# Opening of a fused attention and MLP kernel: replicating four scale vectors on TensorE instead of by DMA, adding beta by extra matmul rows, and loading q by head groups

## The chip, the cores and the metric

The kernel runs on one core of a Trainium2 chip. The metric is the device time of one execution in microseconds. "Span" is the length of the profiled execution, some 1.8 us less than the time of the same run (828.8 and 830.6 for the kernel before). Executions of one kernel on one chip differ by 0.3 to 0.5%. So stages are compared by their times inside the traces, and whole kernels by repeated runs beside the kernel before on the same chip.

## The reference

Eight batches, 16 query heads, 4 key heads, 384 positions, head size 64, model width 1024, hidden width 4096.

```python
scores = scale * np.matmul(q, k.transpose(0, 1, 3, 2))      # k, v repeated over the heads of a group
attn = softmax(scores)
x = np.matmul(attn, v)                                       # -> [8, 384, 1024]
a1 = alpha1 * x + beta1
tok = np.einsum('ts,bsd->btd', w_tok, a1)                    # "token mix"
u = x + lam * tok
a2 = alpha2 * u + beta2
ch = np.maximum(a2 @ w_ch1, 0.0) @ w_ch2                     # h, then ch
return u + lam * ch
```

## The kernel before

The kernel works batch by batch. `main(b)` is the two big products of batch b; `side(b+1)`, the attention and token mix of the next batch, is cut into units that are slipped between the matmuls of `main(b)`. The first batch has nothing to hide behind: `side(0)` runs alone. I call that stretch, up to the first `h` matmul, the **opening**, and `main(0)` with `side(1)` in it the **first big stage**.

The parts that the change touches, with cuts marked:

```python
def bcast(eng, t, ap, lo, hi):                 # one vector to all 128 partitions, by DMA
    src = bass.AP(tensor=ap.tensor, offset=ap.offset + lo, ap=[[0, P], [1, hi - lo]])
    eng.dma_start(out=t[:, lo:hi], in_=src)
# ... in av_piece(p, hh) of the first batch: lam is folded into alpha1 and beta1
nc.vector.tensor_tensor(out=g1[:, r], in0=g1[:, r], in1=lam_t[:, r], op=MUL)
nc.vector.tensor_tensor(out=h1[:, r], in0=h1[:, r], in1=lam_t[:, r], op=MUL)
# ... x = av / sum, then
nc.vector.tensor_tensor(out=t, in0=x[:, :, cols(p)], in1=bc(g1, p), op=MUL)          # L232
eng = nc.gpsimd if first and p < NP - 2 else nc.vector
eng.tensor_tensor(out=a1s[p], in0=t, in1=bc(h1, p), op=ADD)                          # L235
# ... tok(p)
for tt in range(NST):
    for st in range(NST):
        nc.tensor.matmul(out=ps[:, tt, :], lhsT=wtokT[:, st, tt * P:(tt + 1) * P],   # L242
                         rhs=a1s[p][:, st, :], start=(st == 0), stop=(st == NST - 1))
u = x[:, :, cols(p)]
nc.vector.tensor_tensor(out=u, in0=ps, in1=u, op=ADD)                                # L245
nc.vector.tensor_tensor(out=a2s[p], in0=u, in1=bc(al2, p), op=MUL)                   # L247
# ... head of the program
load_k(0)
nc.scalar.dma_start(out=qst, in_=...)          # q, first head group
load_q(0, [0], G)                              # q, the other groups, in pieces of 64 elements
load_q(0, [1, 2], G)
for t, ap in ((g1, moe_alpha1), (lam_t, moe_lam), (h1, moe_beta1)):
    bcast(nc.scalar, t, ap, 0, 256)
    bcast(nc.sync, t, ap, 256, DM)
bcast(nc.sync, al2, moe_alpha2, 0, DM)
for c in range(RING):
    load_w1(c)
```

The softmax here doesn't subtract the row's maximum and nothing guards it: scores larger than these inputs give would overflow.

Of the kernel before, what the change touches and what calls it, by code (L numbers as in the profile page):

```python
# [12 lines left out]
def kernel(  # L13
# [21 lines left out]
    nc = tc.nc  # L35
# [34 lines left out]
    g1, h1, lam_t, al2 = (const.tile([P, DM], f32, tag=n, name=n) for n in ("g1", "h1", "lam", "al2"))  # L70
# [12 lines left out]
    def load_k(b):  # L83
        ks[b] = []
        for h in range(0, Hkv, 2):
            t = sb.tile([P, 2, NST, D], f32, tag="kst", name="kst", bufs=2)
            nc.sync.dma_start(out=t, in_=k[b, h:h + 2].rearrange("h (p st) d -> p h st d", st=NST))
            ks[b].append(t)

    def place_k(b, i):  # L90
        if i == 0:
            k2s[b] = sb.tile([P, NST, Hkv, 2, D], bf, tag="k2", name="k2", bufs=1)
        copies = (nc.vector.tensor_copy, nc.vector.tensor_copy if i else nc.scalar.copy) if b < 2 else [nc.gpsimd.tensor_copy] * 2
        for a in range(2):
            copies[a](out=k2s[b][:, :, 2 * i:2 * i + 2, a, :], in_=ks[b][i].rearrange("p h st d -> p st h d"))
# [5 lines left out]
    def load_q(b, sts=range(NST), i=0):  # L101
        if b not in qrs:
            qrs[b] = sb.tile([P, NST, Hq, D], bf, tag="q_raw", name="q_raw", bufs=1)
        for st in sts:
            nc.gpsimd.dma_start(out=qrs[b][:, st, i:], in_=by_st(q[b])[:, st, i:])
# [8 lines left out]

    def bcast(eng, t, ap, lo, hi):
        src = bass.AP(tensor=ap.tensor, offset=ap.offset + lo, ap=[[0, P], [1, hi - lo]])
        eng.dma_start(out=t[:, lo:hi], in_=src)
# [16 lines left out]
    def tp_ps(shape):  # L134
        return psum.tile(shape, bf, tag="tp", name="tp", bufs=1)
# [6 lines left out]
    def side(b):  # L142
        vb = vt[b % 2]
        x = sb.tile([P, NST, DM], f32, tag="x", name="x", bufs=2)
        xs[b] = x
# [11 lines left out]
        def k_transpose(h0):  # L157
            k2 = k2s[b]
            ps = tp_ps([P, 2 * NST, P])
            for i in range(2 * NST):  # L160
                src = k2[:, i % NST, h0 + i // NST].rearrange("p a d -> p (a d)")
                nc.tensor.matmul(out=ps[:, i, :], lhsT=src, rhs=ident, is_transpose=True,
                                 start=(i == 0), stop=(i == 2 * NST - 1), skip_group_check=True)
            nc.vector.tensor_copy(out=kT[:, :, h0:h0 + 2, :].rearrange("p st h s -> p h st s"),
                                  in_=ps.rearrange("p (h st) s -> p h st s", h=2))

        def q_transpose(g):
            ps = tp_ps([P, 2 * NST, P])
            for i in range(2 * NST):
                h = g * G + 2 * (i // NST)  # L170
                nc.tensor.matmul(out=ps[:, i, :],  # L171
                                 lhsT=qrs[b][:, i % NST, h:h + 2, :].rearrange("p h d -> p (h d)"),
                                 rhs=ident, is_transpose=True, start=(i == 0),
                                 stop=(i == 2 * NST - 1), skip_group_check=True)
            nc.vector.tensor_copy(out=qT[:, :, 2 * g:2 * g + 2, :].rearrange("p st a s -> p a st s"),  # L175
                                  in_=ps.rearrange("p (a st) s -> p a st s", a=2))
# [3 lines left out]
        def scores(i, later=False):  # L180
# [11 lines left out]
            def exp():  # L192
                e = sb.tile([P, 2, 4, P], bf, tag="es", name="es", bufs=EB)
                nc.scalar.activation(out=e, in_=sc, func=EXP, scale=scale_qk)  # L194
                ess[i] = e
# [10 lines left out]
        def av_piece(p, hh):  # L206
# [12 lines left out]
            if hh == 0:  # L219
                if first and p in (0, 2):  # L220
                    r = slice(0, 256) if p == 0 else slice(256, DM)
                    nc.vector.tensor_tensor(out=g1[:, r], in0=g1[:, r], in1=lam_t[:, r], op=MUL)
                    nc.vector.tensor_tensor(out=h1[:, r], in0=h1[:, r], in1=lam_t[:, r], op=MUL)
                return
            rinv = sb.tile([P, 2, NST, 1], f32, tag="rinv", name="rinv", bufs=1)
            nc.vector.reciprocal(out=rinv, in_=av[:, :, :, D:])  # L226
            for hh in range(2):
                c0 = (2 * p + hh) * D
                nc.vector.tensor_tensor(out=x[:, :, c0:c0 + D], in0=av[:, hh, :, :D],  # L229
                                        in1=rinv[:, hh].to_broadcast([P, NST, D]), op=MUL)  # L230
            t = sb.tile([P, NST, P], f32, tag="tmp", name="a1f", bufs=4)
            nc.vector.tensor_tensor(out=t, in0=x[:, :, cols(p)], in1=bc(g1, p), op=MUL)  # L232
            a1s[p] = sb.tile([P, NST, P], bf, tag="a1", name="a1", bufs=2)
            eng = nc.gpsimd if first and p < NP - 2 else nc.vector
            eng.tensor_tensor(out=a1s[p], in0=t, in1=bc(h1, p), op=ADD)  # L235

        def tok(p):
            ps = psum.tile([P, NST, P], f32, tag="av" if first else "sc", name="tok",
                           bufs=1 if first else 2)
            for tt in range(NST):  # L240
                for st in range(NST):
                    nc.tensor.matmul(out=ps[:, tt, :], lhsT=wtokT[:, st, tt * P:(tt + 1) * P],  # L242
                                     rhs=a1s[p][:, st, :], start=(st == 0), stop=(st == NST - 1))
            u = x[:, :, cols(p)]
            nc.vector.tensor_tensor(out=u, in0=ps, in1=u, op=ADD)  # L245
            a2s[p] = sb.tile([P, NST, P], bf, tag="a2", name="a2", bufs=3)
# [15 lines left out]
        def wtok_transpose():  # L262
            wv = wtok_in.rearrange("p tt (s st) -> p tt st s", st=NST)
            for st in range(NST):
                ps = tp_ps([P, NST, P])
                for tt in range(NST):
                    nc.tensor.matmul(out=ps[:, tt, :], lhsT=wv[:, tt, st, :], rhs=ident,
                                     is_transpose=True, start=(tt == 0),
                                     stop=(tt == NST - 1), skip_group_check=True)
                nc.vector.tensor_copy(out=wtokT[:, st, :], in_=ps.rearrange("p a b -> p (a b)"))  # L270
# [10 lines left out]
        if not first:  # L281
            if pe_flip:
# [3 lines left out]
                add(q_transpose, 1)  # L286
            for j in range(NP + 4):
# [3 lines left out]
                if j <= NP:  # L291
                    add(scores2, j)
                    if pe_flip and j in (1, 3):
                        add(q_transpose, 2 + j // 2)
# [8 lines left out]
        add(q_transpose, 0)  # L303
        for i in range(18):
            add(scores, i)
            if i == 1:
                add(q_transpose, 1)
            if i in (5, 9):
                add(q_transpose, i // 4 + 1)
            if i == 4:  # L310
                add(k_transpose, 2)
            if i == 6:
                add(wtok_transpose)
            for p in range(NP):
# [4 lines left out]
                if i == last + 2 and p > 1:  # L319
                    add(tok_flip, p - 2)  # L320
        add(tok, NP - 3)
        add(av_piece, NP - 1, 0)
        add(av_piece, NP - 1, 1)
        add(tok, NP - 2)
        add(a2_transpose, NP - 3)
        add(tok, NP - 1)
        add(a2_transpose, NP - 2)
# [53 lines left out]
    with tc.manual_schedule(engines=order):  # L381

        nc.vector.memset(wtokT, 0.0)
        warm = psum.tile([P, 512], f32, tag="mm", name="warm", bufs=2)
        for _ in range(9):
            nc.tensor.matmul(out=warm[:, :S], lhsT=wtokT[:, 0, :P], rhs=wtokT[:, 1, :],
                             start=True, stop=True)
        load_k(0)
        stage = sb.tile([P, NST, DM], f32, tag="x", name="stage", bufs=2)
        qst = stage[:, 0, :G * NST * D].rearrange("p (h st d) -> p h st d", h=G, st=NST)  # L390
        nc.scalar.dma_start(out=qst, in_=q[0, :G].rearrange("h (p st) d -> p h st d", st=NST))
        load_q(0, [0], G)
        make_identity(nc, ident)
        for t in vt:
            nc.vector.memset(t[:, :, :, D:], 1.0)
        load_q(0, [1, 2], G)
        vst = stage[:, 2, :Hkv * NST * D].rearrange("p (h st d) -> p h st d", h=Hkv, st=NST)
        nc.sync.dma_start(out=vst, in_=v[0].rearrange("h (p st) d -> p h st d", st=NST))
        nc.gpsimd.tensor_copy(out=vt[0][:, :, :, :D], in_=vst.rearrange("p h st d -> p st h d"))
# [3 lines left out]
        load_k(1)  # L403
        for t, ap in ((g1, moe_alpha1), (lam_t, moe_lam), (h1, moe_beta1)):
            bcast(nc.scalar, t, ap, 0, 256)
            bcast(nc.sync, t, ap, 256, DM)
        bcast(nc.sync, al2, moe_alpha2, 0, DM)
        wtok_in = stage[:, 1, :NST * S // 2].bitcast(bf).rearrange("p (tt s) -> p tt s", tt=NST)
        nc.gpsimd.dma_start(out=wtok_in, in_=moe_w_tok.rearrange("(p tt) s -> p tt s", tt=NST))
        be2 = stage[:, 0, DM - NDT:]  # L410
        with nc.allow_non_contiguous_dma(reason="one small vector, once"):
            nc.sync.dma_start(out=be2, in_=moe_beta2.rearrange("(dt di) -> di dt", di=P))
        for c in range(RING):
            load_w1(c)
        loads = {7: [(load_w2, 0, 0, 2)], 25: [(load_q, 1, [0]), (load_q, 1, [1])],
                 31: [(load_q, 1, [2]), (load_v, 1, [0])], 37: [(load_v, 1, [1])], 43: [(load_v, 1, [2])]}
        for i, f in enumerate(side(0)):
# [3 lines left out]
            if i == 4:  # L421
                place_k(0, 1)
# [61 lines left out]
```

## Time and profile before

Three runs: median 829.54 us (828.04 to 830.46).

| stretch of the trace | us |
|---|---|
| opening, up to the first h matmul | 52.0 |
| first h matmul to the sixth (last) output of batch 0 | 104.2 |
| last output of batch 0 to that of batch 6 | 584.8 |
| from there to the end | 87.7 |

The prediction below shows the views that carry the argument. A row of the timeline gives start, duration, engine, line, operation, what it writes and reads, shape and count, and in square brackets the idle time before it with what ended it. One more view is needed later, a token mix at full clock and the instruction after it (timeline, kernel before):

```profile
24.51 0.68 PE L242 MATMUL tok<-a,wtokT 128*128 128x128 bf16 x9
25.12 0.39 PE L188 MATMUL sc<-qT,kT 64*128 64x384 bf16 x4
```

The nine matmuls of one head pair take 0.68 us to the end of the last, and 0.61 us to the start of the next instruction, which overlaps it.

### The profile page before, as it was taken

The page shows a single profiled execution, that of the slowest core. Times are in us where ns is not written, and L with a number is a line of the kernel's source. Part 1 is how long each engine was busy: PE and PEld are TensorE (multiplying, and loading weights), DVE is VectorE, ACT ScalarE, POOL GpSimd, SP SyncE. Part 2 cuts the span into 40 slices and gives each one's busy share as a digit, 9 for nine tenths or more (in the row PEclk, how much of TensorE's full clock was granted, in tenths as well). Part 3 has the DMA queues.
Part 4 walks back from the last instruction along what each step waited for, and adds up shares of the span by engine and source line. Part 5 has one row for each costly group of instructions (what it writes and reads, how often), then busy time and mean ns, then how long its engine had stood idle before and what let it go on. Part 6 is the DMA issues. An engine that isn't in the chain of part 4 may idle for free.

```text
span 828.8 us, 13904 instructions
## 1 busy us (share of the span) xinstructions
PE 797.1 (96%) x5958; PEld 445.9 (54%) x6011; DVE 350.9 (42%) x728; ACT 219.0 (26%) x287; POOL 187.6 (23%) x229
## 2 busy tenths in 40 slices
PE   5679999999999999999999999999999999999997
PEld 2456555566455654556555664556545565556543
DVE  3854645234452445434443344434444344442222
ACT  3514331233103321043211332133310342102100
POOL 5414441033302250022400224012410221003000
PEclk7869999999999999999999999999999999999999
DMA  9999999799948999499917999379995999119701
GB/s 193 230 145 181 200 210 190 138 175 151 140 97 134 176 169 90 97 166 173 169 46 138 181 169 138 82 128 179 174 91 111 130 176 141 37 55 182 97 38 39
DMA packets 265342, 115.09 MB, mean 139 GB/s; under 512 B 113728, under 2 KB 258496, under 8 KB 265280
## 3 DMA queue, kind: packets, MB, share of 16 engines
q0 software_dynamic: 200832, 83.28, 91.2%
q1 hardware_dynamic: 63488, 30.13, 15.6%
q10 hardware_dynamic: 960, 0.79, 0.4%
q8 instruction: 47, 0.77, 0.4%
q14 instruction: 15, 0.12, 0.0%
HBM read 172.56 MB, written 12.58 MB: 223 GB/s over the span
## 4 chain that ended last, share of the span: by engine, by line
PE 92%; DMA 3%; DVE 2%; issue 1%; ACT 1%; POOL 0%; SPq 0%; DVEq 0%; POOLq 0%
PE h L344 41%; PE ch L368 40%; PE av L217 4%; PE sc L188 4%; PE tok L242 4%; DMA q_raw<-in_q_dram 1%; DMA h<-in_moe_beta_dram 1%; DMA a2T<-a 1%; DVE a L247 1%; ACT hT L352 0%; DVE x L229 0%; DVE x L245 0%; DVE a1f L232 0%; PE tp L171 0%; PE tp L257 0%
## 5 line engine op out<-in xcount | busy, mean ns | idle before, releaser
L344 PE MATMUL h<-a2T,w 128*128 128x384 bf16 (+1 forms) x2048 | 356.6, 327 | 1.2 <-DVE bias L350 0.2
L368 PE MATMUL ch<-w,hT 128*128 128x512 bf16 x1483 | 345.1, 379 | 3.5 <-issue 1.1
L344 PEld LDWEIGHTS <-w 128*128 128x128 bf16 x2048 | 192.9, 98 | 129.4 <-issue 10.6
L127 POOL DMA_DIRECT2D w<-in_moe_w_ch_dram x128 | 112.3, 879 | 549.3 <-PE h L344 514.3
L368 PEld LDWEIGHTS <-hT 128*128 128x128 bf16 x1536 | 142.6, 98 | 155.6 <-issue 4.4
L194 ACT ACTIVATE es<-sc 128x1024 bf16<-128x1024 f32 x144 | 141.2, 1021 | 302.9 <-PE sc L188 302.9
L354 DVE TENSOR_SCALAR hT<-h,bias 128x384 bf16<-128x384 f32 x128 | 78.9, 617 | 186.1 <-PE h L344 185.5
L352 ACT ACTIVATE hT<-h,bias 128x384 bf16<-128x384 f32 x128 | 74.3, 581 | 229.6 <-PE h L344 202.6
L373 DVE TENSOR_TENSOR o<-ch,lam 128x512 f32<-128x512 f32 x48 | 33.0, 688 | 96.9 <-PE ch L368 96.9
L245 DVE TENSOR_TENSOR x<-tok,x 128x384 f32<-128x384 f32 x64 | 35.5, 555 | 82.9 <-PE tok L242 82.9
L217 PEld LDWEIGHTS <-es 128*128 128x128 bf16 x1152 | 52.4, 99 | 23.1 <-issue 1.6
L217 PE MATMUL av<-v,es 128*128 128x65 bf16 x1152 | 56.8, 196 | 0.8 <-ACT es L194 0.6
L242 PE MATMUL tok<-a,wtokT 128*128 128x128 bf16 x576 | 45.0, 226 | 8.8 <-DVE x L245 8.7
L242 PEld LDWEIGHTS <-wtokT 128*128 128x128 bf16 x576 | 38.9, 101 | 22.8 <-issue 6.5
L188 PE MATMUL sc<-qT,kT 64*128 64x384 bf16 (+2 forms) x576 | 46.5, 278 | 0.7 <-DVE qT L175 0.7
L229 DVE TENSOR_TENSOR x<-av,rinv 128x192 f32<-128x192 f32 x128 | 39.8, 352 | 2.3
L247 DVE TENSOR_TENSOR a<-x,al 128x384 bf16<-128x384 f32 x64 | 38.2, 597 | 3.2 <-DMA a2T<-a 1.0
L226 DVE RECIPROCAL rinv<-av 128x6 f32<-128x6 f32 x64 | 12.3, 192 | 59.5 <-PE av L217 59.3
L232 DVE TENSOR_TENSOR a1f<-x,g 128x384 f32<-128x384 f32 x64 | 36.0, 563 | 2.4
L188 PEld LDWEIGHTS <-kT 64*128 64x128 bf16 x576 | 20.1, 95 | 28.0 <-issue 23.6
L374 DVE TENSOR_TENSOR o<-o,x 128x512 f32<-128x512 f32 x48 | 33.2, 692 | 1.6
L235 DVE TENSOR_TENSOR a<-a1f,h 128x384 bf16<-128x384 f32 x58 | 32.5, 561 | 2.2
(38 smaller groups left out, 127.9 us busy)
## 6 DMA issues: line engine op xcount, KB each, us to landing
w<-in_moe_w_ch_dram POOLq DMA_DIRECT2D x135, 512.0 KB, 7.6
out_dram<-o SPq DMA_DIRECT2D x48, 256.0 KB, 2.2
q_raw<-in_q_dram POOLq DMA_DIRECT2D x21, 256.0 KB, 8.8
kst<-in_k_dram SPq DMA_DIRECT2D x16, 192.0 KB, 2.8
w<-in_moe_w_ch_dram POOLq DMA_DIRECT2D x10, 256.0 KB, 12.1
w<-in_moe_w_ch_dram POOLq DMA_DIRECT2D x1, 2048.0 KB, 35.0
v<-in_v_dram POOLq DMA_DIRECT2D x21, 64.0 KB, 8.8
a2T<-a SPq DMA_TRANSPOSE x53, 3.3
```

Source lines behind the costliest of these rows:

```text
L127: nc.gpsimd.dma_start(out=t, in_=w1src[:, :, c * CW * P:(c + 1) * CW * P])
L188: nc.tensor.matmul(out=sc[:, hh, k % 4:k % 4 + n], lhsT=kT[r, sk, 2 * p // G, :], rhs=qT[r, st:st + n, p, :], start=True, stop=True)
L194: nc.scalar.activation(out=e, in_=sc, func=EXP, scale=scale_qk)
L217: nc.tensor.matmul(out=av[:, hh, sq, :], lhsT=ess[k // 4][:, hh, k % 4, :], rhs=vb[:, sk, hk, :], start=(sk == 0), stop=(sk == NST - 1))
L229: nc.vector.tensor_tensor(out=x[:, :, c0:c0 + D], in0=av[:, hh, :, :D], in1=rinv[:, hh].to_broadcast([P, NST, D]), op=MUL)
L232: nc.vector.tensor_tensor(out=t, in0=x[:, :, cols(p)], in1=bc(g1, p), op=MUL)
L242: nc.tensor.matmul(out=ps[:, tt, :], lhsT=wtokT[:, st, tt * P:(tt + 1) * P], rhs=a1s[p][:, st, :], start=(st == 0), stop=(st == NST - 1))
L247: nc.vector.tensor_tensor(out=a2s[p], in0=u, in1=bc(al2, p), op=MUL)
L344: nc.tensor.matmul(out=ps[:, :n], lhsT=w1[:, dt, j * P:(j + 1) * P], rhs=a2T[:, dt, :n], start=(dt == 0), stop=(dt == NDT - 1))
L352: nc.scalar.activation(out=hT[:, nt, :], in_=ps[:, :S], func=RELU, bias=c1)
L354: nc.vector.tensor_scalar(out=hT[:, nt, :], in0=ps[:, :S], scalar1=c1, scalar2=0.0, op0=ADD, op1=mybir.AluOpType.max)
L368: nc.tensor.matmul(out=ps, lhsT=hT[:, nt, ms * P:(ms + 1) * P], rhs=w2[:, nt, cs], start=(nt == 0), stop=(nt == NNT - 1))
```

## The change

The intent is to end the opening's waits for q and for the replicated vectors. The vectors come as 24 rows (eight 128-element pieces, three copies). VectorE splits them into three bf16 parts whose sum is the f32 value (`split`); TensorE multiplies a 0/1 selector with them and so writes the f32 vectors to all partitions (`spread`). beta1 (the prediction calls it LN1's beta) goes into the token mix as three extra rows of the contraction: R holds the row sums of the token weights (two bf16 parts), H the beta (bf16 parts). q is loaded by head groups in pieces of 192 elements. The first batch keeps its temporaries in the unused hidden activations, and copies move to ScalarE and GpSimd. The core of the diff, cut:

```diff
-    def bcast(eng, t, ap, lo, hi): ...
+        def rows_r():                       # R: row sums of the token weights, two bf16 parts
+            for st in range(NST):
+                nc.tensor.matmul(out=ps[:3], lhsT=ones3, rhs=wtokT[:, st, :], start=(st == 0), ...)
+            nc.vector.tensor_copy(out=t, in_=ps[:3])
+            nc.vector.scalar_tensor_tensor(out=R, in0=t, scalar=neg3, in1=ps[:3], op0=MUL, op1=ADD)
+        def spread(ps_, vs, tag, eng="ACT"):
+            for i, p in enumerate(ps_):
+                nc.tensor.matmul(out=ps[:, i * w:(i + 1) * w], lhsT=sel[:, p:p + 1].to_broadcast([24, P]),
+                                 rhs=rows_b[:, vs[0] * P:vs[1] * P], start=True, stop=True)
+            evac(eng)(out=vecs[:, ...], in_=ps[:, ...])
@@ tok(p)
+                if first:
+                    nc.tensor.matmul(out=ps[:, tt, :], lhsT=R[:, tt * P:(tt + 1) * P],      # L250
+                                     rhs=H[:, cols(p)], start=False, stop=True)
@@ av_piece
+            if first:                       # one VectorE op, no beta
+                nc.vector.tensor_tensor(out=a1s[p], in0=x[:, :, cols(p)], in1=bc(g1, p), op=MUL)
@@ side(1)
+            for p in range(0, NP if b == 1 else 0, 2):
+                add(spread, (p, p + 1), (2, 4), "tp")          # lam and beta for the later batches
@@ side(0)
+        at = {1: [(warmup, 3), (split,)], 2: [(warmup, 3), (place_q4, 1, nc.vector), (q_transpose, 2, 2, "DVE", "av"),
+                                             (spread, (0, 1), (0, 2), "tp")], ...}
@@ head of the program
+        load_q4(1)                          # q by head groups, GpSimd's queue
+        nc.sync.dma_start(out=vst, in_=v[0]...)
+        for i, ap in enumerate((moe_alpha1, moe_alpha2, moe_beta1, moe_lam)):
+            nc.sync.dma_start(out=rows_f[:, i * P:(i + 1) * P], in_=...)    # 24 rows of 128
+        place_q4(2, nc.gpsimd); place_k(0, 1); place_q4(3, nc.gpsimd)
+        for c in range(RING - 1):           # the weights' loads, behind GpSimd's copies
+            load_w1(c)
```

## The prediction

> **What bounds the kernel now.** I read the page first, then the chain of waits in order of time up to 110 us, then busy time by stretches, then the timeline of the first 62 us and the groups of lines inside it. The page's second part (40 slices of 20.7 us) says where the lost time lies:
>
> ```profile
> PE   5679999999999999999999999999999999999997
> PEclk7869999999999999999999999999999999999999
> ```
>
> TensorE is 90% busy or more from the fourth slice on; only the first three slices (0 to 62 us) are thin, and there the granted clock is low as well. The stretches agree: between 150 and 750 us TensorE is busy 99.4 us in every 100. So eight passes of the two big matrix products are bound by TensorE, and only the opening, the attention of the first batch that has no other batch's products to hide behind, can give time back. The chain of waits, in order of time, shows the opening's end:
>
> ```profile
> 3.98 10.29 DMA q_raw<-in_q_dram
> ...
> 17.61 9.60 DMA h<-in_moe_beta_dram
> ...
> 30.05 1.09 DVE a L247
> ...
> 37.87 8.32 DMA a2T<-a
> ...
> 51.74 0.50 PE tp L257 x3
> 52.24 5.56 PE h L344 x24
> ```
>
> (start, duration, what.) The first big product waits for the last transposed piece at 52.2 us; before it lie a 10.29 us wait for q, a 9.60 us wait for the vector beta1 copied to all partitions, a VectorE chain, and an 8.32 us transposing transfer. From 52.2 on the remaining (828.8 - 52.2)/8 = 97.1 us per batch are TensorE's. Thus: new time = old time - (52.2 - new start of the first product) + whatever is added after it.
>
> Busy time by stretches of 5 us (PE, PEld, DVE, ACT, POOL busy; then granted clock, DMA share, GB/s):
>
> ```profile
> 10.00:15.00 5.00, 0.70 (x9) 0.49 (x10) 0.03 (x1) 0.00 (x0) 4.21 (x5) 0.50 1.29 183
> 25.00:30.00 5.00, 1.83 (x36) 1.18 (x33) 3.66 (x7) 2.66 (x3) 0.28 (x1) 1.00 1.50 262
> 30.00:35.00 5.00, 4.32 (x52) 2.78 (x52) 4.83 (x12) 2.96 (x3) 2.60 (x3) 0.66 1.39 202
> 45.00:50.00 5.00, 2.77 (x32) 2.35 (x30) 3.72 (x9) 0.48 (x1) 0.00 (x0) 0.50 2.70 148
> ```
>
> From 10 to 15 nothing but GpSimd's issuing works: everybody waits for q. From 30 to 40 VectorE is over 93% busy: it is the bound there. From 45 the tail is a ping-pong of VectorE and TensorE at half clock. The timeline shows why VectorE is slow in the middle:
>
> ```profile
> 33.12 0.99 POOL L235 TENSOR_TENSOR a<-a1f,h 128x384 bf16<-128x384 f32 x1 [2.40 <-PE av L217]
> 33.45 1.07 DVE L247 TENSOR_TENSOR a<-x,al 128x384 bf16<-128x384 f32 x1
> ...
> 43.47 0.56 DVE L247 TENSOR_TENSOR a<-x,al 128x384 bf16<-128x384 f32 x1
> ```
>
> The same multiplication takes 1.07 us while GpSimd adds beta, and 0.56 us when GpSimd is quiet.
>
> **What the Trainium skill says.** (1) "GPSIMD Engine Reference", section 1 Specifications: GpSimd's SBUF interfaces are shared with VectorE, with contention for VectorE instructions that have two SBUF inputs. The trace agrees: L247 (two SBUF inputs) 1.07 against 0.56 us, while L245 (one input in PSUM) keeps 0.55 us. (2) "TensorE: Matmul & The Clock Gate", Part 1: an idle window of about 3.4 us puts the array at half clock, some 3.4 us of busy time bring it back. The trace agrees: clock 0.50 in 10:15, and the nine token-mix matmuls (L242) take 0.68 us at 24.5 and 1.14 us at 33.5, after TensorE had idled from 26.8 to 30.1. (3) "DMA: Bandwidth & Descriptors", Specifications: at least 512 B for line rate. The trace agrees in kind: from 6 to 8 us, when q arrives in pieces of 64 elements, 2344 of 2379 packets are under 512 B and 162 GB/s move; from 4 to 6, with long pieces, 333 GB/s.
>
> **The change part by part.**
>
> Removed transfers. The four vectors are no longer replicated by DMA: 4 x 512 KB = 2.1 MB, 10.6 us at the 197 GB/s of this stretch. Instead four transfers of 24 x 128 f32 (12 KB each). The wait for lam and beta1 (17.6 to 27.2) goes, and with it four VectorE products of 0.41, 0.42, 0.96, 0.96 us. In exchange VectorE does a split into bf16 parts early: two products on 24x128 (about 0.2 each) and five operations on 24x512. The cast of 384 f32 took 0.43, so 512 take some 0.56; 3 x 0.56 + 2 x 0.6 + 0.4 = 3.3 us, 3.5 with gaps. This is ON the path, since it stands ahead of the copies and attention results in VectorE's queue.
>
> Spreading. Eight TensorE products and four ScalarE copies of 512 f32 ahead of the first product. ScalarE's row: 1024 elements 1.02 us, 384 elements 0.48, so 512 take 0.6: 2.4 us. Three q/k copies of 768 (about 0.81 each) also move from VectorE to it. ScalarE sum in the opening: 2 x 0.51 + 18 x 1.02 + 2.4 + 2.4 = 24.2 us. The queue order confirms these places.
>
> q by head groups. Pieces of 192 elements rather than 64, a third of the packets. Only two groups are needed for the first work; the stall to 14.3 us ends. GpSimd gets three or so copies near 1 us at 6 to 14 us, so the first w1 loads go out near 13.5 instead of 8.7. Five w1 tiles (2.6 MB), w2 (2.1), q and v (1.0) need 5.7/0.197 = 29 us, to about 43, much as before (about 52) by the removed 2.1 MB. So no new weight starvation.
>
> LN1 beta. GpSimd's six additions (6.0 us) and VectorE's two (1.1) go; twenty-four K=3 matmuls come, about 0.1 us each, 2.4 us of TensorE, and 0.8 us of VectorE for the row of sums. L247 falls from a mean of 0.857 to 0.56: 8 x 0.3 = 2.4 us less on VectorE. VectorE per head pair: 0.19 + 0.62 + 0.56 + 0.55 + 0.56 = 2.5 us.
>
> Buffers and order. The first batch keeps its exponentials (six instead of four), a1 (three for two) and a2 (five for three) in the still unused hidden activations. That removes the wait of L247 for a transposing transfer (1.0 us). Six warming matmuls are added, in gaps. Each token mix is queued two score steps later, so that its a1 is ready; the price is that more of them are left for the tail.
>
> Walking the new queues with these durations: q and k transposed by 6.6; split 7.0 to 10.5; second q group placed and transposed by 12.0; first attention product done 12.7 (before: 17.3); weights of the token mix and its row sums done 16.5; first token mix 17.0 to 17.9 (before 24.5, evacuated only at 29.5 to 30.0). From there ScalarE sets the pace: its remaining 15 exponentials and copies, 15 x 1.02 + 3 x 0.6 + 2.4 = 19.5 us after 12.4, plus about 2.5 of waits, end at 34.4. Then the tail: two token mixes, the last attention product, its 1.4 us on VectorE, token mix 0.9, two VectorE operations 1.1, transpose 0.4: about 41.2. If TensorE ran at half clock from 30 on, I get 45. I choose 42.5, nearer the first, since the queues leave no TensorE gap of 3 us.
>
> Added afterwards: eight spreading products in the first batch's big stage. Six 128-column products cost 0.34 us there, so 256 columns cost 0.11 each: 0.9 us on the path; the ScalarE copies are hidden.
>
> Sum: 829.5 - (52.2 - 42.5) + 0.9 = 820.7; I say 820.5.
>
> **The rivals.** (a) The transposing transfers take the place of the removed wait. The fifth, for head pair 4, is issued near 33.5 and, at the 8.2 us of before, lands near 41.7, as late as my chain. For: DMA stays saturated to 43 us. Against: in the kernel before it was hidden by the last pieces too. If it takes 12 us, the start is 45.5 and the time 824. (b) VectorE stays the bound: its work after 12.7 is 8 x 2.5 + 1.9 = 21.9 us, end at 34.6 if never idle, so it has some 6 us of slack; if the split meets GpSimd's copies and doubles, add 3 us: 823.5. (c) Buffers and in-order queues: one transpose bank is now shared by transposes, row sums and spreads that ScalarE empties behind exponentials; each late copy stalls all of TensorE, which can go cold. That makes 45 to 47, time 823 to 826. (d) Better than walked: attention and token mix overlap fully, start at 37, time 815.
>
> **Range and chances.** Starts from 38.5 to 46.5 give 816.5 to 824.5; I widen the top to 825. Faster by over 2% needs 813, that is a start below 35, at the point where ScalarE's own work would just end: 0.04. Slower by 2% has no source, as all later work is unchanged: 0.01. Else within 2%: 0.95.
>
> **What would show it.** Right: first h matmul at 40 to 45 us; no wait for a vector's DMA after 17 us; L258 (the former L247) near 0.56 us throughout; q stall below 3 us; clock 1.0 from 15 to 35; the same 97 us per batch later, plus 1 us in the first. Wrong: a fifth transposing transfer as the last releaser of the first h matmul; split over 5 us; PEclk at 0.5 in the middle; or TensorE waiting for w1 between 42 and 100 us, because the weights now leave GpSimd 5 us later.

## The result, and the profile after

Four runs of the changed kernel: median 830.32 us (829.19 to 830.71), against 829.75 us (828.04 to 830.46, four runs) of the kernel before. The ratio is 1.0008, 95% interval 0.9989 to 1.0026: no change. A ratio here is the mean time of one kernel's runs over that of the other's of the same rounds, so it is not quite the ratio of the medians that I quote. The gain of 1% did not come; 830.3 lies above the range.

The same two rows of the page's second part, changed kernel:

```profile
PE   5889999999999999999999999999999999999997
PEclk7989999999999999999999999999999999999999
```

TensorE is fuller than before in the second and third slices, and the clock is better in the second. The opening did become shorter, but by little:

| stretch, us | before | changed | changed, again |
|---|---|---|---|
| first h matmul starts | 52.04 | 48.82 | 49.34 |
| first h to sixth output of batch 0 | 104.24 | 106.80 | 106.88 |
| sixth output of batch 0, at | 156.28 | 155.62 | 156.22 |
| last output of batch 6 to the end | 87.7 | 88.4 | 87.7 |

(The third column is a control run described below.) So 2.7 to 3.2 us are won in the opening instead of 9.7, and the first big stage gives 2.6 of them back instead of 0.9. The batches between are equal to 0.1 us.

Where the opening stalls, by stretches of 5 us (columns as in the prediction: PE, PEld, DVE, ACT, POOL busy; then clock, DMA share, GB/s):

```profile
10.00:15.00 5.00, 0.00 (x0) 0.00 (x0) 4.79 (x8) 0.23 (x1) 4.51 (x5) 0.63 0.20 26
15.00:20.00 5.00, 4.95 (x46) 2.86 (x47) 2.37 (x7) 2.69 (x4) 4.98 (x6) 0.50 1.01 121
20.00:25.00 5.00, 5.00 (x62) 2.77 (x61) 3.71 (x10) 2.89 (x4) 0.00 (x0) 0.85 1.42 218
...
30.00:35.00 5.00, 5.00 (x68) 3.21 (x68) 2.98 (x7) 4.07 (x6) 3.90 (x4) 1.00 1.53 188
```

From 10 to 15 us TensorE is now wholly idle while VectorE and GpSimd work; then it runs at half clock. From 30 to 35 it is the only full engine. Two things are new: DMA moves 26 GB/s from 10 to 15, because GpSimd copies before it issues the weights; and the bound of the middle seems to have passed from VectorE to TensorE (e3 below tests it). The timeline of the changed kernel names the pieces:

```profile
9.96 0.48 DVE L472 TENSOR_TENSOR hT<-hT 24x128 f32<-24x128 f32 x2 [2.56 <-DMA hT<-in_moe_lam_dram]
...
10.93 1.19 DVE L476 SCALAR_TENSOR_TENSOR hT<-hT,stage 24x512 f32<-24x512 bf16 x1
...
13.70 0.93 DVE L479 CAST hT<-hT 24x512 bf16<-24x512 f32 x1
...
15.02 0.82 PE L174 MATMUL tp<-ident,q_raw 128*128 128x128 bf16 x6 [5.58 <-DVE q_raw L452]
...
22.76 0.33 PE L246 MATMUL tok<-hT,wtokT 128*128 128x128 bf16 x3
...
23.02 0.23 PE L250 MATMUL tok<-stage 3*128 3x128 bf16 x1
...
23.18 0.34 PE L246 MATMUL tok<-hT,wtokT 128*128 128x128 bf16 x3
...
24.04 0.39 PE L190 MATMUL sc<-qT,kT 64*128 64x256 bf16 x4
...
24.74 0.56 DVE L258 TENSOR_TENSOR hT<-x,vecs 128x384 bf16<-128x384 f32 x1
...
45.34 0.43 PE L246 MATMUL tok<-hT,wtokT 128*128 128x128 bf16 x3 [0.88 <-DVE hT L234]
```

The split starts at 9.96, when the row of lam lands, not at 7.0; it ends at 14.63, not 10.5; and TensorE idles 5.58 us behind it, since VectorE places q after it. In the token mix, one beta matmul starts at 23.02 and the next ordinary one at 23.18: it holds TensorE for 0.16 us, though it has three rows. From its start to that of the next instruction a token mix takes 1.28 us (22.76 to 24.04) against 0.61 before: 0.48 more for the three beta matmuls, and 0.19 because the ordinary ones beside them run slower. As predicted, the multiplication by alpha2 (L258) takes 0.56 us throughout, now that it no longer meets GpSimd's additions.

The last line is from the opening's tail. The clock was back at 1.00 from 22 us on, and here it falls again: 0.71 from 45 to 46 us, then 0.50 until 52. TensorE had not idled for longer than these 0.88 us since 20 us. In a second profile of the same kernel (c0 below) it fell near 42.6 us, after no idle stretch over 0.70 us.

### The profile page after: what moved, and what is told of

It reads as the page before. It is cut to its first block, busy times and chain, and to the rows that moved or that the text cites. A ratio compares the mean times of both kernels' runs of the same rounds, so it can differ in the third digit from the quotient of the medians.

```text
span 828.8 us, 14029 instructions
## 1 busy us (share of the span) xinstructions
PE 804.6 (97%) x6007; PEld 446.3 (54%) x6060; DVE 349.3 (42%) x731; ACT 225.4 (27%) x298; POOL 185.3 (22%) x229
## 4 chain that ended last, share of the span: by engine, by line
PE 39%; issue 38%; POOL 9%; DMA 1%; DVE 1%; ACT 0%; POOLq 0%; DVEq 0%
PE ch L402 20%; PE h L378 14%; POOL w L126 7%; PE av L222 1%; PE tok L246 1%; PE sc L190 1%; DMA w<-in_moe_w_ch_dram 1%; POOL q_raw L108 1%; POOL v L102 1%; POOL k L98 1%; ACT hT L386 0%; PE tp L268 0%; POOLq L126 0%; DVE a1f L237 0%; DVE a L239 0%
## 5 line engine op out<-in xcount | busy, mean ns | idle before, releaser
L199 ACT ACTIVATE es<-sc 128x1024 bf16<-128x1024 f32 x126 | 123.4, 1021 | 286.7 <-PE sc L190 286.7
L407 DVE TENSOR_TENSOR o<-ch,vecs 128x512 f32<-128x512 f32 x48 | 33.0, 688 | 93.9 <-PE ch L402 93.9
L222 PEld LDWEIGHTS <-es 128*128 128x128 bf16 x1008 | 45.9, 97 | 21.4 <-ACT es L199 0.9
L222 PE MATMUL av<-v,es 128*128 128x65 bf16 x1008 | 49.2, 193 | 0.8 <-ACT es L199 0.8
L246 PEld LDWEIGHTS <-wtokT 128*128 128x128 bf16 x576 | 37.3, 98 | 15.8 <-issue 3.2
L246 PE MATMUL tok<-a,wtokT 128*128 128x128 bf16 x504 | 37.3, 219 | 0.0
L258 DVE TENSOR_TENSOR a<-x,vecs 128x384 bf16<-128x384 f32 x56 | 31.4, 561 | 1.9
L239 DVE TENSOR_TENSOR a<-a1f,vecs 128x384 bf16<-128x384 f32 x56 | 31.2, 558 | 2.2
L237 DVE TENSOR_TENSOR a1f<-x,vecs 128x384 f32<-128x384 f32 x56 | 31.2, 558 | 2.0
```

The lines of the kernel that those rows point to most:

```text
L199: nc.scalar.activation(out=e, in_=sc, func=EXP, scale=scale_qk)
L222: nc.tensor.matmul(out=av[:, hh, sq, :], lhsT=ess[k // 4][:, hh, k % 4, :], rhs=vb[:, sk, hk, :], start=(sk == 0), stop=(sk == NST - 1))
```

## The experiments

All edits are to the changed kernel unless said otherwise. "First h" is the start of the first h matmul, "stage" the time from there to the sixth output of batch 0. The ratio is to the kernel before on the same chip.

| run | first h | stage | span | ratio (95%) |
|---|---|---|---|---|
| before / changed | 52.0 / 48.8 | 104.2 / 106.8 | 828.8 / 828.8 | 1.0008 (0.9989 to 1.0026) |
| e1 rows first | 48.2 | 106.9 | 827.6 | 0.9974 (0.9959 to 0.9989) |
| e2 keep warm | 47.9 | 107.3 | 827.6 | 0.9982 (0.9964 to 1.0000) |
| e3 no beta rows (wrong) | 44.9 | 106.6 | 823.9 | 0.9940 (0.9925 to 0.9955) |
| e4 q before split | 48.4 | 107.1 | 827.9 | 0.9992 (0.9975 to 1.0009) |
| e5 spread late | 59.4 | 106.3 | 838.2 | 1.0089 (1.0048 to 1.0130) |
| e6 tail warm | 48.3 | 105.1 | 826.0 | 0.9964 (0.9950 to 0.9979) |
| e7 lam, beta1 by DMA | 48.3 | 108.0 | 828.6 | 0.9989 (0.9972 to 1.0005) |
| e9 e1, e2 and e3 together (wrong on purpose) | 42.0 | 111.0 | 825.5 | one look |
| e10 beta rows padded to 128 | 45.6 | 106.7 | 824.7 | 0.9953 (0.9938 to 0.9968) |
| e11 all mended | 42.9 | 113.2 | 828.6 | 0.9987 (0.9970 to 1.0003) |
| e12 kernel before, tail warm | 51.5 | 103.6 | 827.6 | one look |
| e13 e11, w2 later | 42.9 | 105.4 | 820.8 | 0.9904 (0.9880 to 0.9928) |
| e14 e10 and e6 | 45.0 | 106.0 | 823.5 | 0.9930 (0.9911 to 0.9950) |
| e15 w2 later alone | 48.4 | 107.9 | 828.8 | one look |

### e1: vector rows first

```diff
-        nc.sync.dma_start(out=vst, in_=v[0]...)            # ahead of the four row loads
+        nc.sync.dma_start(out=vst, in_=v[0]...)            # behind them
```

> Edit: the four small transfers of the vector rows are issued ahead of v instead of behind it; nothing else. Theory (the split into bf16 parts stands ahead of everything and starts late, at 9.96 us, because the last vector row lands so late): the split starts by 7.7 us, TensorE's empty stretch (9.4 to 15.0 us) shrinks to under 3 us, the clock stays 1.0 from 10 to 20 us, and the first h matmul starts at 43 to 45 us instead of 48.8; time 824.5 to 827. Rival (the opening is limited by how fast all its inputs arrive, so moving one ahead delays the others): split earlier, but v or q late, first h at 47.5 us or later and time within 1.5 us of the changed kernel.

The split started at 9.06 instead of 9.96 and, with fewer of GpSimd's copies beside it, took 3.9 us instead of 4.7. TensorE's empty stretch shrank to 3.7 us and the clock stayed 1.0, yet the first h came only 0.6 us earlier. The theory missed: lam still landed 4.6 us after its issue had ended, so the order of issue was not the main thing that made it late, and an end of the split 1.7 us earlier was not worth 4 to 5 us. The rival's signs all came: v, now behind, released GpSimd's copy of it only at 11.59 us instead of 6.29, the first h came after 47.5 and the time stayed within 1.5 us. That the arrival of all inputs is what limits the opening does not follow: e3 below gains 4 us without touching a transfer.

### e2: TensorE kept warm in the first gap

```diff
-        at = {..., 2: [(warmup, 3), (place_q4, ...
+        at = {..., 2: [(warmup, 30), (place_q4, ...
```

> Edit: 30 warming matmuls instead of 3 in the stretch in which TensorE waits for the second q group (9.4 to 15.0 us); no work is moved. Theory (half clock is a cost of its own): clock 1.0 from 15 to 22 us, first attention product done by 17.3 us instead of 18.0, row sums R done by 21 instead of 22.7, first h matmul at 46.5 to 47.3 us instead of 48.8. Rival (VectorE and ScalarE set the pace, the clock is a symptom): first h at 48.4 us or later.

The clock held 1.0 from 10 us on; R was done at 21.05 (22.70); first h at 47.9, 0.9 us earlier and half of what was expected. TensorE then waited 0.64 us for H's transfer in its first token mix, a wait that the changed kernel does not have. Half clock is a cost of its own, but only part of a gain made before 22 us is kept after it.

### e3: no beta rows

```diff
-                if first:
+                if False:                                   # the 24 matmuls R x H
```

> Edit: the 24 three-row matmuls that add beta in the token mix are left out (the result is wrong on purpose by the beta1 term). Theory (TensorE itself is the bound from 20 to 40 us, and each token mix now takes 1.3 us instead of 0.68): the first h matmul starts 2.5 to 4 us earlier, 45 to 46.5 us. Rival, my prediction's walk (ScalarE's exponentials set the pace there): first h less than 1.2 us earlier, 47.6 us or later.

First h at 44.87, 3.95 us earlier; the rival, my own walk with ScalarE as the pace, allowed 1.2. A token mix now takes 0.60 us to the next start (22.44 to 23.04) instead of 1.28, so each of the 24 matmuls had cost 0.23 us, its effect on its neighbours counted, and all together some 5.5 us. Of these 3.95 lay on the path: TensorE bounds the greater part of the middle of the changed opening. Timeline of e3:

```profile
22.44 0.66 PE L246 MATMUL tok<-hT,wtokT 128*128 128x128 bf16 x9
23.04 0.39 PE L190 MATMUL sc<-qT,kT 64*128 64x256 bf16 x4
```

The check of the result passed this run all the same: beta1 and lam are drawn some 0.01 in size, and the missing term, a product of the two, is evidently too small for it. So where a run below is called right, that rests on its edit keeping the sum, not on the check alone.

### e4: q placed before the split

```diff
-        at = {1: [(warmup, 3), (split,)], 2: [(warmup, 3), (place_q4, 1, ...), (q_transpose, ...), (spread, ...)],
+        at = {1: [(warmup, 3)], 2: [(warmup, 3), (place_q4, 1, ...), (q_transpose, ...), (split,), (spread, ...)],
```

> Edit: on VectorE the placing of the second q group and its transposes come ahead of the split; the spread stays behind the split. Theory (TensorE starves because q waits behind the split): transposes of group 1 near 9.5 us instead of 15.0; but TensorE's next piece, the spread, still waits for the split's end near 14.5, so there remains a gap of 4 us and the gain is small: first h at 47 to 48.3 us. Rival (only the place of the copies matters, the spread does not): first h at 44 to 46 us.

The transposes ran at 9.16 us, but the spread, next in TensorE's queue, still waited 5.24 us for the split. First h at 48.39, just outside the expected top of 48.3 and far from the rival.

### e5: the spread moved behind the second attention product

```diff
-        at = {1: [..., (split,)], 2: [..., (spread, (0, 1), (0, 2), "tp")], ..., 5: [(wtok_transpose, 2, "tp"), (rows_r,)], 6: [spread (2, 3)], ...
+        at = {..., 5: [(wtok_transpose, 2, "tp"), (split,)],
+              6: [(spread, (0, 1), (0, 2), "tp"), (scale, 0), (scale, 1), (rows_r,), (spread, (2, 3), (0, 2), "tp")], ...
```

> Edit: the second q group is placed and transposed ahead of the split, and the first spread, the a1 of head pairs 0 and 1 and the row sums R move behind the second attention product, so that nothing on TensorE waits for the split until about 17 us. Theory (the late start of the opening, 4.5 us behind my walk, is what the split and the spread cost): no TensorE gap over 3 us before 20 us, clock 1.0 throughout, fourth exponential starts by 11 us instead of 16.95, first h matmul at 44 to 45.5 us instead of 48.8, time down 3 to 4.5 us from the changed kernel. Rival (after 22 us TensorE with its beta rows sets a pace that an earlier start cannot change): first h at 47 us or later.

This went the other way: first h at 59.4. The fourth exponential did start at 11.5, but I had put the split behind the copies of the token weights, so it ran from 14.0 to 18.15; TensorE waited 3.67 us for it, then 1.31 us for R, then 2.42 us for H's transfer. The clock fell and did not come back (stretches of e5):

```profile
20.00:25.00 5.00, 1.27 (x9) 0.62 (x7) 1.55 (x4) 0.58 (x1) 0.00 (x0) 0.50 1.42 204
25.00:30.00 5.00, 5.00 (x50) 3.27 (x48) 2.49 (x6) 2.63 (x3) 0.00 (x0) 0.50 1.61 207
...
35.00:40.00 5.00, 5.00 (x34) 2.28 (x31) 1.34 (x3) 3.52 (x5) 4.33 (x5) 0.50 1.30 172
```

From 25 to 40 us the profile calls TensorE busy all the time, and still the granted clock is 0.50. The run says nothing for or against the late start. Not all of its 10.6 us is the clock's: the three waits come to 7.4 us, against 5.6 us for the one wait of the changed kernel. But three of its four executions took 839 to 840 us at a mean clock of 0.973 and one took 832.7 us at 0.985, so the same program took some 7 us less where the mean clock was higher.

### e6: TensorE kept warm in the opening's tail

```diff
+        add(warmup, 3)
         add(tok, NP - 2)
 ...
+        add(warmup, 8)
         add(tok, NP - 1)
+        add(warmup, 8)
```

> Edit: 19 warming matmuls in the three waits of TensorE in the opening's last 8 us; no work moves. Theory (the end of the opening and the first 5.6 us of h run at half clock only because TensorE waits there): clock 1.0 from 40 to 55 us; first h at 48.0 to 48.4 us instead of 48.8, and its first 24 matmuls take about 4 us instead of 5.8, in sum 2 to 2.8 us. Rival (the clock is not held by so few, or the warming work delays the last pieces): no change or up to 1 us slower.

As expected: clock 1.0 from 40 to 55, first h at 48.32, and its first 24 matmuls in 4.08 us where the changed kernel took 5.78 (timeline of e6, then of the changed kernel):

```profile
48.32 4.08 PE L381 MATMUL h<-a2T,w 128*128 128x385 bf16 x24
```

```profile
48.82 5.78 PE L378 MATMUL h<-a2T,w 128*128 128x385 bf16 x24
```

The span fell by 2.7 to 2.8 us. The work is the same.

### e7: lam and beta1 replicated by DMA again, late

```diff
-            for p in range(0, NP if b == 1 else 0, 2):
-                add(spread, (p, p + 1), (2, 4), "tp")
+            for t, ap in ((h1, moe_beta1), (lam_t, moe_lam)):        # in late_loads()
+                nc.sync.dma_start(out=t, in_=...)                     # 512 KB each
+        nc.vector.tensor_tensor(out=h1, in0=h1, in1=lam_t, op=MUL)    # before main(0)
```

> Edit: lam and beta1 for the later batches come by two replicating transfers, issued near 16 us, and the four spread pairs in the first batch's big stage go. Theory (these spreads and their place cost what the big stage of the first batch lost): from the first h matmul to the sixth output of batch 0 it takes 104.2 to 105.0 us instead of 106.8 (before: 104.2); first h unchanged within 0.5 us. Rival (the stage is longer because it starts earlier and the weights or the second batch's attention come too late): still 106.2 us or more.

By its total the rival's number came: 108.0. But the trace shows two causes laid over each other. TensorE waited 2.3 us for q of batch 1 near 57 to 59 us, a wait the changed kernel does not have, and ran the first hidden blocks at half clock longer. From the eighth hidden block to the sixth output, after the spreads' place, it took 90.0 us. This figure separates the runs in which I read it: 89.9 to 90.1 in every kernel without spreads in the stage (before, e7, e11, e12, e13), and 92.1 in the kernels with them (changed, its control, e3, e6, e10, e14, e15); only e9, described below, has 93.9, with 1.4 us of waits for w1 in it. So with the spreads 2.2 us more fall after the eighth block. Up to there the changed kernel takes 14.5 us, the kernel before 14.1: the spreads (1.3 us) stand in place of two units of transposes and one of scores (1.2 us), which run later. These 1.2 us are the larger part of the 2.2; 0.8 more is one wait of an attention product for its exponentials, which neither the kernel before nor e7 has.

### c0: the changed kernel again

No edit.

> The changed kernel once more, unedited, as a control for the last batch: in its first profile the last batch took 88.4 us from the sixth output of batch 6 to the end, with a wait of 0.3 us for w1, against 87.7 before. If that is chance it takes 87.6 to 87.8 here; if it belongs to the change, 88.2 or more.

The last batch took 87.7 us: the wait of the first profile was chance. What belongs to the change ends with batch 0, where it was level with the kernel before (156.22 against 156.28 us).

### e9: rows first, warm, and no beta rows

```diff
 # the edits of e1, e2 and e3
```

> Edits of three earlier runs together: vector rows first, TensorE kept warm, no beta rows (wrong on purpose). Theory (the 6.3 us by which the first h matmul came later than my walk are the beta rows, 4.0 us, and the late and cold start, about 1 to 2 us, and they add): first h at 42.5 to 44 us instead of 48.8 or 49.3, my walk's 42.5 nearly reached. Rival (they hide one another or something else bounds): 44.6 us, about the run without beta rows alone, or later.

First h at 42.00 us, where my walk had 42.5 (and 41.2 without the margin), and below the 42.5 to 44 expected here. The gains do not hide one another: 0.6, 0.9 and 3.95 us singly, 6.8 together. Of these, 2.87 come on top of e3 and stand for the late and cold start. But the span fell only to 825.5, since new waits came in the first big stage (who TensorE waited for in e9, 42 to 154 us: total us, times, longest):

```profile
PE tp L174 <- DMA q_raw<-in_q_dram: 2.3, 2, 1.4
PE h L378 <- DMA w<-in_moe_w_ch_dram: 1.4, 2, 0.8
PE h L378 <- DMA a2T<-hT: 1.4, 1, 1.4
```

All three are transfers: q of batch 1, w1, and the transposing transfer of the opening, my rival (a). The last one means that the first h is an early mark here: after four of its matmuls TensorE waited 1.36 us for the fifth transposed piece.

### e10: beta rows padded to 128

```diff
-        R = stage[:3, 2120:2312].bitcast(bf)
-        H = stage[:3, 2312:2824].bitcast(bf)
+        R, H = stage[:, 2120:2312].bitcast(bf), stage[:, 2312:2824].bitcast(bf)
+        nc.gpsimd.memset(stage[:, 2120:2824], 0.0)          # rows 3 to 127 stay zero
```

> Edit: R and H are padded with zeros from 3 to 128 rows, so the same 24 beta matmuls run in the same shape as their neighbours; the count stays, the result is right. Theory (what costs is not the count but the change between 3-row and 128-row weights, which keeps the next weights from loading behind the running product): a token mix takes 0.85 to 0.9 us instead of 1.3, first h 2 to 3 us earlier than 48.8 to 49.3, that is 46 to 47.2. Rival (each extra matmul costs 0.165 us whatever its shape): no change, 48.5 or later.

```profile
23.04 0.33 PE L246 MATMUL tok<-hT,wtokT 128*128 128x128 bf16 x3
23.21 0.22 PE L250 MATMUL tok<-stage 128*128 128x128 bf16 x1
23.26 0.33 PE L246 MATMUL tok<-hT,wtokT 128*128 128x128 bf16 x3
```

(Timeline of e10.) The beta matmul now holds TensorE 0.05 us (23.21 to 23.26) instead of 0.16, and a token mix takes 0.76 us to the next start (23.04 to 23.81), against 0.60 without beta rows and 1.28 with three-row ones. So the same 24 matmuls, zeros included, cost a quarter. First h at 45.58, even earlier than expected, and the result is right and 0.5% faster than before. What cost was the change of shape. The records of the weight loads (PEld) agree with the theory's reason, in the changed kernel and then in e10:

```profile
23.02 0.09 PEld L250 LDWEIGHTS <-stage 3*128 3x128 bf16 x1
23.17 0.17 PEld L246 LDWEIGHTS <-wtokT 128*128 128x128 bf16 x3
```

```profile
23.16 0.10 PEld L250 LDWEIGHTS <-stage 128*128 128x128 bf16 x1
23.21 0.21 PEld L246 LDWEIGHTS <-wtokT 128*128 128x128 bf16 x3
```

With three rows a weight load begins only when its own product does (23.02 and 23.02, 23.17 and 23.18), at both changes of shape. In e10 it begins 0.05 us earlier, while the product before it runs (23.16 for 23.21, 23.21 for 23.26). Why the hardware does so no record here tells.

### e11: everything mended

```diff
 # e1, e2 and e10; the four spreads of lam and beta go into the tail, with warming matmuls:
+        add(spread, (0, 1), (2, 4), "sc")
+        add(warmup, 2)
         add(tok, NP - 2)
 ...
+        add(spread, (2, 3), (2, 4), "sc")
         add(a2_transpose, NP - 2)
+        add(spread, (4, 5), (2, 4), "sc")
+        add(warmup, 4)
         add(tok, NP - 1)
+        add(spread, (6, 7), (2, 4), "sc")
+        add(warmup, 5)
```

> Edits together, result right: vector rows first, TensorE kept warm in the wait for q, beta rows padded to 128, and the four spreads of lam and beta moved from the first big stage into the waits of the opening's tail, where they and eleven warming matmuls also hold the clock. Theory: first h at 44.5 to 46 us, the big stage of batch 0 from first h to sixth output back to 102 to 102.8 us (104.2 in the kernel before, less 1.9 that half clock costs its first 24 matmuls), so 819.5 to 822 us profiled span and about 1% faster than before. Rival (the weights' transfers then become the bound of the first big stage, as q of batch 1 did when lam and beta1 were replicated by transfers): the stage takes 104.5 us or more and the span is 823 or more.

First h at 42.92, and the whole gain was lost again: 828.6. The wait list of e11 from 43 to 157 us:

```profile
PE tp L174 <- DMA q_raw<-in_q_dram: 7.7, 3, 4.8
```

q of batch 1 landed from 53 to 57 us, and TensorE waited 7.7 us for its three parts. The rival had the mechanism, though it was q rather than the weights that came late.

### e12: the kernel before, with a warm tail

```diff
 # kernel before
+        add(warmup, 14)
         add(tok, NP - 3)
 ...
+        add(warmup, 10)
         add(tok, NP - 1)
         add(a2_transpose, NP - 2)
+        add(warmup, 5)
```

> The kernel BEFORE with 29 warming matmuls in its own tail waits (41 to 52 us). Theory (half clock at the end of the opening is a common loss of both kernels, not a thing of the change): first h at 50.5 to 51.7 instead of 52.04, its first 24 matmuls 4 us instead of 5.8, span 825.5 to 826.8 instead of 828.8. Rival (the clock cannot be held there): 828 or more.

Clock 1.0 from 40 to 55, first h at 51.5, span 827.6: a gain of 1.2 us, less than the expected 2 to 3.3. TensorE then waited 0.88 us for the fifth transposing transfer. Half clock at the opening's end is a loss of both kernels, worth less in the kernel before.

### e13: e11 with part of w2 loaded later

```diff
-        loads = {9: [(load_w1, RING - 1), (load_w2, 0, 0, 2)], ...
+        loads = {9: [(load_w1, RING - 1), (load_w2, 0, 0, 4)], ...      # 1 MB instead of 2 MB
-            if b == 0 and 2 <= c < 12:
-                load_w2(*((0, 6 + c, 16) if c < 10 else (1, c - 10, 16)))
+            if b == 0 and c < 12:
+                load_w2(0, 4 + c, 16)
-                for i in range(1, 8):
+                for i in range(8):
```

> Edit to e11_all_mended: of the 2 MB of w2 loaded ahead of q of batch 1, 1 MB is loaded later in eighths, during the first big stage. Theory (q of batch 1 sits behind w2 in one queue and the earlier opening now reaches it first): q lands about 5 us earlier, its waits of 7.65 us shrink to under 2.7, first h unchanged at 42.9, span 821.5 to 824. Rival (transfers as a whole are at their limit, so that w2 or w1 comes late instead): waits for w appear, span 826 or more.

First h unchanged at 42.91; the wait for q fell to 2.3 us (wait list of e13, 43 to 149 us), no wait for weights over 0.2 us appeared, and the clock rows of the page are full from the first slice:

```profile
PE tp L174 <- DMA q_raw<-in_q_dram: 2.3, 1, 2.3
```

```profile
PE   7889999999999999999999999999999999999997
PEclk9999999999999999999999999999999999999999
```

Median 822.8 us against 831.28 of the kernel before in the same rounds, ratio 0.9904 (0.9880 to 0.9928): better than both kernels, and right. The span of 820.8 was slightly below what either account gave.

### e14: beta rows padded and a warm tail

```diff
 # the edits of e6 and e10
```

> Edits to the changed kernel: beta rows padded to 128 (e10) and TensorE warm in the tail (e6), nothing else. If the two add: first h at 45.0 to 45.4 us, its first 24 matmuls at full clock, span 821.8 to 822.8 (828.7 less 4.0 less 2.7). Rival: q of batch 1, needed from about 54.5 us, has not landed, and up to 2 us of waits take the place, span 823 to 825.

First h at 45.01 and span 823.5, which by its number is the rival's. But its cause is not: there was no wait for q, only one of 0.75 us for a transposing transfer. Up to that wait the two gains add.

### e15: w2 later in the changed kernel itself

```diff
 # the edit of e13, applied to the changed kernel
```

> The same move of 1 MB of w2 in the changed kernel itself, unmended. Theory (there q lands in time, as the opening ends at 49 us): no gain, span 828.2 to 829.0, first h 48.8 to 49.4. Rival (the transfers already held the changed kernel back): 827.5 or less.

Span 828.8, first h 48.42. q landed 15.6 us after issue (median) instead of 19.8, and the end did not move: the first hidden blocks ran at half clock longer (their first 24 matmuls took 6.82 us instead of 5.78), which took the 0.4 us of the earlier start and more. In the changed kernel as given the transfers were not yet the bound.

## Why the prediction was wrong

Two steps of the walk failed. One is "**From there ScalarE sets the pace**". For the greater part TensorE did. I had booked the beta rows as "about 0.1 us each, 2.4 us of TensorE", beside the path. They cost 0.23 us each, their effect on the neighbours counted, 5.5 us in all, and leaving them out brought the first h 3.95 us forward (e3). The error was of size and of place: my list of work per head pair had VectorE and ScalarE in it, but not TensorE.

The other is "**split 7.0 to 10.5**" with "**the queues leave no TensorE gap of 3 us**". The split ran from 9.96 to 14.63. It waited 2.56 us for the row of lam, and it ran longer beside GpSimd's copies (1.19 us for an operation that took 0.74 without them in e1). The gap was 5.58 us and the clock half until about 22 us. Late and cold start together measured 2.87 us (44.87 to 42.00, e9 against e3). These points of the walk can be read in the traces:

| us | walk | changed | e9 |
|---|---|---|---|
| split ends | 10.5 | 14.6 | 13.0 |
| first attention product done | 12.7 | 18.0 | 15.8 |
| first token mix starts | 17.0 | 22.8 | 20.1 |
| ScalarE's last exponential ends | 34.4 | 40.6 | 35.8 |
| first h matmul | 42.5 | 48.8 | 42.0 |

The two measured terms add to 6.8 us, and 6.3 lie between the walk and the changed kernel, but that they agree so well is partly luck. The changed kernel was 5.8 us late when its first token mix began, before any beta matmul, and needed 26.1 us from there, the walk 25.5. e9 was still 3.1 us late there, and needed 21.9. So the walk had booked the way from the first token mix 3.6 us too long (2.3 without its margin), and this hid most of what the beta rows cost. e9 reached the walk's end by two errors that cancel.

The measure by which I judged the clock failed too. A tail without a gap of 3 us was to keep it up; in the changed kernel it fell near 45.4 us after no idle stretch over 0.88 us, and e6 prices this at 2.7 us. My reading of the kernel before had passed over a sign of it: the token mix at 30.07, right after the gap of 3.2 us, still took 0.68 us.

The next step is "**Added afterwards ... 0.9 us on the path**". The stage became 2.6 us longer. The pairs cost 0.32 us each where they stand, 1.3 us, and 0.8 us is the wait of an attention product for its exponentials that came with the shift of the other units (e7). The rest, some 0.5 us, I did not take apart.

The last could not show itself in the changed kernel: "**So no new weight starvation**", with q and v landed at about 43. q landed from 50 to 54 us (issued 31.1 to 34.5, 19.8 us to landing), v after it. I had left out the transfers of k, the transposing transfers and the 4 us of idle DMA while GpSimd copies, and had taken 197 GB/s for the whole way, where 99 to 148 moved from 46 to 54 us (stretches of 2 us). e9 shows what my opening would have met, since its loads and spreads stand where the changed kernel has them: waits of 2.3 us for q of batch 1, 1.4 for w1 and 1.4 for the fifth transposed piece, and 827.3 us in one look, still above the range. So rival (a), a transfer in the place of the removed wait, was the right kind, but with q of batch 1 as its main transfer.

What held: TensorE bounds everything after batch 0, whose later batches stayed equal; the waits for a vector's transfer after 17 us and for the last q groups' transfers went; the multiplication by alpha2 takes 0.56 us; and no version of the changed kernel moved the time by 2%.

The sum, in spans: expected -9.7 + 0.9 = -8.8 us. The opening missed by 6.3, the stage by 1.7, and chance in the last batch of the first profile added 0.7; that is 8.7, and the measured change was 0.0.

## What to carry to other kernels

When work moves between engines, list every engine's time per unit of work, including the one that receives a few small instructions: twenty-four tiny matmuls were worth 4 us here. Keep the shape of weights constant in a stream of matmuls, padding with zeros if need be, and fill TensorE's short waits with harmless matmuls where the clock would fall. Short waits can be enough to lose it. Before you shorten a stage, look up when the next stage's data lands: in e11 the first h came 5.9 us earlier and the end did not move, until e13 changed the order of the loads.

## What the Trainium skill lacked or had wrong

- No page gives a time for changing the row count within a stream of matmuls. "TensorE: Matmul & The Clock Gate", section Why this matters for your kernels, says that a single K=32 matmul takes the same time as one with K=128, and singly these agree (0.23 us with 3 rows, 0.22 with 128). "TensorEngine Tiling (Array Packing)", section Tiling Modes, says that a change of tiling mode drains TensorE, without a figure; the traces do not name the mode. Here a 3-row matmul among 128-row ones added 0.23 us to a token mix and a zero-padded 128-row one 0.05 (changed kernel and e10 against e3; first h 48.8, 45.6 and 44.9 us).
- "TensorE: Matmul & The Clock Gate", Part 1, has the clock back after some 3.4 us of busy time. In e5 the profile shows TensorE busy 5.00 of 5.00 us in three stretches from 25 to 40 us with the clock at 0.50; in the changed kernel it did come back near 22 us. Nor did its fall need an idle stretch of such a length: 0.88 us was the longest before the fall at 45.4 us in the changed kernel. Busy as the profile counts it is not enough to tell. Filling TensorE's waits of 0.6 to 1.3 us in the tail won 2.7 us (e6).
- "DMA: Bandwidth & Descriptors", section Rules for kernel authors, says that a leading zero-stride broadcast of c copies confines a transfer to at most c engines; the vector rows are such transfers, with c = 3. It gives no time for it. Here 12 KB took about 5 us: lam's issue ended at 4.96 and the split, which waited for it, began at 9.96; issued ahead of v it came only 0.9 us sooner (e1). Whether the three engines or the full queue are the cause no run here shows.
